# Packing w_in by chunk with mirrored blocks, and folding the row DFT twice, in a fused spectral and gated-MLP kernel

## The chip, the cores and the metric

The kernel runs on one core of one Trainium2 chip. The metric is the device time of one execution in microseconds (us), median over timed executions. TensorE is called PE in the profile, its weight loads PEld, VectorE is DVE, ScalarE is ACT, GpSimd is POOL, and SyncE, which issues most DMAs, is SP. A PSUM tile is a buffer that this kernel's matmuls write and another engine reads out before it is written again. A line number such as L477 is a line of that version's source, so the same statement has different numbers in different versions.

## The reference, cut to what matters

```python
xn = layernorm(x)                          # x is 2048 x 576, bf16
s  = irfft2(rfft2(xn) * W)                 # spectral branch, W is 2048 x 289, complex
z  = gelu(xn @ w_in)                       # w_in is 576 x 4608
z1, z2 = z[:, :2304], layernorm(z[:, 2304:])
g  = w_sp @ z2 + b_sp[:, None]             # w_sp is 2048 x 2048
out = x + s * silu((z1 * g) @ w_out)       # w_out is 2304 x 576
```

The change touches the layernorm of `x`, the first step of `rfft2` (a DFT along the 576 columns), the product with `w_in`, and one place in the last phase.

## The kernel before: the parts that matter

The 2048 rows are handled in 16 groups of 128, which this document calls rows 0 to 15. For each row DVE computes the layernorm, the normalized row is transposed (on PE for rows 0 to 6, by DMA from row 7 on) into `xnT`, DVE folds it, and PE does the DFT products, with chunks of `xn @ w_in` between them to keep PE filled. The 576 columns are two halves of H = 288; each half is cut into two blocks of 128 and a tail of 32, so `xnT` has five column blocks.

```python
# the first loads (cut)
for a, eng in enumerate((nc.sync, nc.scalar)):        # row 0, in two halves, on two queues
    eng.dma_start(out=XC[0][:, 0, a * H2:(a + 1) * H2], in_=xv[:, 0, a * H2:(a + 1) * H2])
load_win_main(*wh[0], nc.scalar, (0,))                # w_in for chunk 0: pieces, 768-byte runs
nc.scalar.dma_start(out=ident[:], in_=cd_id.ap())     # identity for the PE transposes
load_win_main(*wh[1], nc.scalar, (0,))
load_win_main(*wh[0], nc.sync, (1,))
load_row(1)
load_row(2)
...
def ln1_apply(m):                                     # DVE: one instruction of 512 columns, one of 128
    nc.vector.tensor_scalar(out=xn[:, 0:4 * P]..., in0=xr[:, :, 0:2 * P]..., scalar1=mean, scalar2=rs, ...)
    nc.vector.tensor_scalar(out=xn[:, 4 * P:KS * P]..., in0=xr[:, None, :, 2 * P:H2]..., ...)

def p0_fold(m):                                       # DVE: column j plus and minus column j + H
    xe, xo = xnT[:, m, 0:KS - 1:2, :], xnT[:, m, 1:KS - 1:2, :]
    nc.vector.tensor_tensor(out=FS[m % 4][:, 0, :, :], in0=xe, in1=xo, op=ALU.add)
    nc.vector.tensor_tensor(out=FS[m % 4][:, 1, :, :], in0=xe, in1=xo, op=ALU.subtract)

def p0(m, start):                                     # PE: four matmuls of 2 * LE = 290 columns
    for par in range(2):                              # even and odd frequencies
        for k in range(2):                            # two blocks of 128
            nc.tensor.matmul(p0_ps[m][:, par, 0:2 * LE], lhsT=FS[m % 4][:, par, k, :], rhs=CDSD[:, par, k, :], ...)
...
# the loop over rows (cut): DVE works ahead of PE
for m in range(MT):
    if m > 1: p0_fold(m)
    if m + 5 < MT: ln1(m + 5)                         # statistics
    if m + 4 < MT: ln1_apply(m + 4)
    ...                                               # PE: chunks of xn @ w_in; p0(m, ...)
...
# the gating phase, one unit (cut): `later` holds the last row's finish, g*y and then +x, on DVE
prod(b, "P6", tb[u, 0])
add(p1a, b, p1)
while later:
    later.pop()()
tsum(u + 1, 0)
...
add(p1, b, p1b)
u_sum(1, 1, c, p1)                                    # frees the PSUM tile c
```

## Time and profile before

The time before is 493.46 us (median of 3 runs, 493.25 to 493.56). The head of its profile page reads as follows. The busy line gives the busy time of each engine, its share of the span, and its number of instructions; the line with percentages alone is the chain of work that ended last, by engine; the last line is DMA traffic by packet size.

```profile
span 491.6 us, 9285 instructions
...
PE 483.9 (98%) x3407; PEld 306.1 (62%) x3407; DVE 331.7 (67%) x739; ACT 159.8 (33%) x335; POOL 206.4 (42%) x272
...
DMA packets 94605, 72.13 MB, mean 147 GB/s; under 512 B 45920, under 2 KB 86752, under 8 KB 94304
...
PE 96%; DVE 1%; ACT 1%; DMA 1%; issue 0%; SPq 0%; DVEq 0%
```

PE bounds the kernel. So a saved PE column is worth its time, unless PE then waits for something.

The start is the one stretch where PE waits. This is PE's timeline of the kernel before: start, duration, engine, line, operation, count, and in brackets the idle time in front and what ended it.

```profile
1.21 3.68 PE L756 MATMUL pw<-Z_74 128*128 128x512 bf16 x9 [1.21 <-DVE Z_74 L220]
5.98 0.44 PE L320 MATMUL pt<-ident,AR 128*128 128x128 bf16 x5 [1.09 <-DMA ident<-c_id]
6.25 0.38 PE L761 MATMUL pw<-Z_74 128*128 128x512 bf16 x1
7.25 0.82 PE L477 MATMUL ph<-AR 128*128 128x384 bf16 x4 [0.62 <-DVE AR L324]
```

Nine warm-up matmuls, row 0's transposes as soon as the identity has landed, and the first chunk of `xn @ w_in` (L477) at 7.25 us.

```profile
32.31 0.66 PE L348 MATMUL pa<-AR 128*128 128x290 bf16 x4
...
33.58 0.67 PE L348 MATMUL pa<-AR 128*128 128x290 bf16 x4
...
36.69 0.66 PE L348 MATMUL pa<-AR 128*128 128x290 bf16 x4
...
37.95 0.67 PE L348 MATMUL pa<-AR 128*128 128x290 bf16 x4
```

PE is busy without a gap, DVE for 6.56 of 10 us (4.82 of the first five, 1.74 of the last). From start to start the 290-column matmuls take 122 to 134 ns. DVE's fold of row 9 ends 2.15 us before its product starts; that distance, DVE's lead over PE, is 0.41 us at row 3, 2.98 at row 8, 2.15 at row 9, 3.37 at row 10 and 2.75 at row 11.

One more place: in the last phase, the finish (multiply and add, L695 and L696) sits on DVE in front of the add that frees a PSUM tile, and PE loses about 0.3 us between the matmuls at 417.94 and 419.08 us.

```profile
416.80 0.45 DVE L695 TENSOR_TENSOR AR<-AR 128x576 bf16<-128x576 bf16 x1
...
417.28 0.81 DVE L696 TENSOR_TENSOR AR<-AR 128x576 bf16<-128x576 bf16 x1
...
419.08 1.03 PE L636 MATMUL pm<-AR 128*128 128x256 bf16 x8
```

### The profile page before, as it was taken

The page shows a single profiled execution, that of the slowest core. Times are in us where ns is not written, and L with a number is a line of the kernel's source. Part 1 is how long each engine was busy: PE and PEld are TensorE (multiplying, and loading weights), DVE is VectorE, ACT ScalarE, POOL GpSimd, SP SyncE. Part 2 cuts the span into 40 slices and gives each one's busy share as a digit, 9 for nine tenths or more (in the row PEclk, how much of TensorE's full clock was granted, in tenths as well). Part 3 has the DMA queues.
Part 4 walks back from the last instruction along what each step waited for, and adds up shares of the span by engine and source line. Part 5 has one row for each costly group of instructions (what it writes and reads, how often), then busy time and mean ns, then how long its engine had stood idle before and what let it go on. Part 6 is the DMA issues. An engine that isn't in the chain of part 4 may idle for free.

```text
span 491.6 us, 9285 instructions
## 1 busy us (share of the span) xinstructions
PE 483.9 (98%) x3407; PEld 306.1 (62%) x3407; DVE 331.7 (67%) x739; ACT 159.8 (33%) x335; POOL 206.4 (42%) x272
## 2 busy tenths in 40 slices
PE   7999999999999999999999999999999999999996
PEld 3555454555556444566666677666666678888885
DVE  6995378798876989856656627666566426877632
ACT  4777777867767565200000111000000011000001
POOL 3681134424533794455354301553553312666600
PEclk9999999999999999999999999999999999999999
DMA  8878899978574999851111896111211872111212
GB/s 272 243 138 201 232 314 274 346 222 225 158 247 113 259 265 252 263 177 33 47 50 34 173 184 170 45 33 34 64 33 39 170 173 70 56 44 44 71 37 61
DMA packets 94605, 72.13 MB, mean 147 GB/s; under 512 B 45920, under 2 KB 86752, under 8 KB 94304
## 3 DMA queue, kind: packets, MB, share of 16 engines
q1 hardware_dynamic: 88832, 57.88, 45.6%
q0 software_dynamic: 4896, 13.17, 8.3%
q8 instruction: 26, 0.43, 0.4%
q10 hardware_dynamic: 832, 0.50, 0.3%
q14 instruction: 19, 0.16, 0.1%
HBM read 40.40 MB, written 21.26 MB: 125 GB/s over the span
## 4 chain that ended last, share of the span: by engine, by line
PE 96%; DVE 1%; ACT 1%; DMA 1%; issue 0%; SPq 0%; DVEq 0%
PE pm L636 44%; PE ph L477 15%; PE ph L573 14%; PE po L690 13%; PE pa L348 2%; PE pb L405 2%; PE pa L421 1%; PE pa L447 1%; PE pa L369 1%; PE pl L690 1%; PE pa L393 1%; DMA AR<-in_A_x_dram 1%; PE pa L440 0%; PE pa L340 0%; PE pt L320 0%; ACT AR L353 0%
## 5 line engine op out<-in xcount | busy, mean ns | idle before, releaser
L636 PE MATMUL pm<-AR,Z_74 128*128 128x384 bf16 (+1 forms) x864 | 138.8, 308 | 0.0
L640 DVE TENSOR_TENSOR AR<-pm,AR 128x384 f32<-128x384 f32 (+3 forms) x162 | 82.4, 513 | 73.4 <-PE pm L636 69.8
L636 PEld LDWEIGHTS <-Z_74 128*128 128x128 bf16 x864 | 84.5, 98 | 40.6
L636 PE MATMUL pm<-AR 128*128 128x384 bf16 (+1 forms) x648 | 107.0, 308 | 0.1
L477 PE MATMUL ph<-AR 128*128 128x384 bf16 (+1 forms) x480 | 87.2, 327 | 0.7 <-DVE AR L324 0.6
L573 PE MATMUL ph<-AR 128*128 128x512 bf16 (+1 forms) x360 | 84.7, 379 | 0.0
L636 PEld LDWEIGHTS <-AR 128*128 128x128 bf16 x648 | 63.4, 98 | 30.7 <-issue 0.3
L650 ACT ACTIVATE AR<-pm 128x384 f32<-128x384 f32 (+1 forms) x27 | 12.3, 455 | 185.3 <-PE pm L636 185.3
L690 PE MATMUL po<-AR 128*128 128x288 bf16 x540 | 66.6, 286 | 0.0
L690 PEld LDWEIGHTS <-AR 128*128 128x128 bf16 x594 | 56.9, 98 | 13.9
L477 PEld LDWEIGHTS <-AR 128*128 128x128 bf16 (+1 forms) x480 | 39.6, 97 | 38.7 <-issue 16.7
L624 POOL TENSOR_TENSOR AR<-Z_74,AR 128x1024 bf16<-128x1024 bf16 x26 | 55.3, 2126 | 12.8 <-PE pm L636 11.4
L651 POOL TENSOR_TENSOR AR<-AR 128x384 f32<-128x384 f32 (+1 forms) x27 | 22.9, 849 | 81.0 <-ACT AR L650 78.4
L593 POOL DMA_DIRECT2D Z1d<-AR x55 | 32.0, 583 | 56.8 <-ACT AR L582 54.5
L582 ACT ACTIVATE AR<-ph 128x512 bf16<-128x512 f32 x72 | 41.9, 596 | 19.8 <-PE ph L573 19.6
L573 PEld LDWEIGHTS <-AR 128*128 128x128 bf16 (+1 forms) x360 | 30.3, 97 | 27.6 <-issue 4.1
L496 ACT ACTIVATE Z_74<-ph 128x384 bf16<-128x384 f32 x72 | 33.6, 499 | 20.1 <-PE ph L477 19.7
L654 POOL TENSOR_TENSOR AR<-AR 128x384 f32<-128x384 f32 (+1 forms) x27 | 30.3, 1123 | 11.8 <-DVE AR L640 11.8
L693 ACT ACTIVATE AR<-po 128x576 bf16<-128x576 f32 x15 | 9.8, 651 | 76.7 <-PE po L690 76.7
L695 DVE TENSOR_TENSOR AR<-AR 128x576 bf16<-128x576 bf16 (+2 forms) x18 | 7.6, 424 | 39.9 <-ACT AR L693 39.9
L647 DVE TENSOR_TENSOR AR<-AR 128x384 bf16<-128x384 bf16 (+1 forms) x108 | 31.7, 334 | 0.9
L395 DVE TENSOR_TENSOR AR<-pa,AR 128x578 bf16<-128x578 f32 x32 | 22.8, 752 | 6.4 <-PE pa L393 3.9
(188 smaller groups left out, 457.6 us busy)
## 6 DMA issues: line engine op xcount, KB each, us to landing
Z1d<-AR POOLq DMA_DIRECT2D x55, 128.0 KB, 4.1
AR<-Z1d SPq DMA_DIRECT2D x36, 192.0 KB, 3.0
AR<-in_A_x_dram SPq DMA_DIRECT2D x19, 144.0 KB, 3.1
AR<-in_B_w_in_dram SPq DMA_DIRECT2D x14, 192.0 KB, 3.8
AR<-in_B_w_out_dram SPq DMA_DIRECT2D x1, 2592.0 KB, 11.5
AR<-Ad SPq DMA_DIRECT2D x4, 578.0 KB, 7.8
AR<-in_A_w_r_dram SPq DMA_DIRECT2D x16, 144.5 KB, 3.9
AR<-in_A_w_i_dram SPq DMA_DIRECT2D x16, 144.5 KB, 3.8
```

What stands on the lines that cost most here:

```text
L477: nc.tensor.matmul(self.ph[:], lhsT=xnT[rows, self.m, ks, :], rhs=WIN2[rows, ks, n * ZC:(n + 1) * ZC], start=start, stop=stop)
L496: nc.scalar.activation(out=zc, in_=ph[:], func=ACT.Gelu_apprx_tanh)
L573: nc.tensor.matmul(self.ph[:].rearrange("p (a t) -> p a t", a=4), lhsT=wb[rows, ks, (fi % WG) * P:(fi % WG + 1) * P], rhs=xnT[rows, 4 * tq ...
L582: nc.scalar.activation(out=zs, in_=ph[:], func=ACT.Gelu_apprx_tanh)
L593: (nc.sync if place[0] > len(kinds) - 16 else nc.gpsimd).dma_start(out=d, in_=s_)
L624: (nc.gpsimd if u else nc.vector).tensor_tensor(out=t, in0=zblk(p, 1, 0), in1=t2, op=ALU.subtract)
L636: nc.tensor.matmul(dst, lhsT=z[:, s, :], rhs=SLB[SA[name]][:, s, 0:nt], start=(s == 0 and not more), stop=(s == HM - 1), skip_group_check= ...
L640: nc.vector.tensor_tensor(out=out, in0=x, in1=y, op=ALU.add)
L647: nc.vector.tensor_tensor(out=o, in0=o, in1=zb[:, f, h, 0:nt], op=ALU.mult)
L651: nc.gpsimd.tensor_tensor(out=p1b, in0=p1, in1=B[1], op=ALU.add)
L654: nc.gpsimd.tensor_tensor(out=ux, in0=p1a, in1=B[0], op=ALU.add)
L690: nc.tensor.matmul(pv[:, hh, :], lhsT=U[:, fi, h, i * P:(i + 1) * P], rhs=WOUT[:, fi, c0 + hh * H2:c0 + hh * H2 + w // nh], start=(fi == 0 ...
```

## The change

The intent has three parts. First, the host lays `w_in` out by chunks of 384 columns, so that one chunk is one DMA with runs of 3840 bytes per partition, where it took up to six DMAs with runs of 768 bytes (of 1536 where two chunks came together). Second, the second block of each half is mirrored (column H-1-i in place of 128+i). A DFT along mirrored pairs splits once more: the sum of a pair needs the cosine columns alone for even frequencies, the difference the sine columns, and the other way round for odd ones. So from row 8 on DVE folds a second time, and PE multiplies by 145 columns in each of its four matmuls instead of 290. Third, some things were moved: the order of the first loads, half of row 1's statistics, the statistics of row 6, and the finish in the last phase.

```diff
+def pack_w_in(w, zc=384):
+    D, F = w.shape
+    H = D // 2
+    nt_ = H - 2 * P
+    i = np.arange(P)
+    rows = np.stack([i, H + i, H - 1 - i, 2 * H - 1 - i, i // nt_ % 2 * H + P + i % nt_], axis=1)
+    return np.ascontiguousarray(w[rows].reshape(P, rows.shape[1], F // zc, zc).transpose(2, 0, 1, 3))
 ...
-    for a, eng in enumerate((nc.sync, nc.scalar)):
-        eng.dma_start(out=XC[0][:, 0, a * H2:(a + 1) * H2], in_=xv[:, 0, a * H2:(a + 1) * H2])
-    load_win_main(*wh[0], nc.scalar, (0,))
+    load_win2(0, nc.scalar)                      # one DMA of 480 KB
     nc.scalar.dma_start(out=ident[:], in_=cd_id.ap())
-    load_win_main(*wh[1], nc.scalar, (0,))
-    load_win_main(*wh[0], nc.sync, (1,))
-    load_row(1)
-    load_row(2)
-    load_win_main(*wh[1], nc.sync, (1,))
+    nc.scalar.dma_start(out=WIN2[:, 1, 0:3, :], in_=B_w_in[NZC + 1, :, 0:3, :])
+    for m in range(3):
+        load_row(m)
+    nc.sync.dma_start(out=WIN2[:, 1, 3:KS, :], in_=B_w_in[NZC + 1, :, 3:KS, :])
 ... (the later loads likewise, one DMA per chunk)
     def ln1_apply(m):
-        nc.vector.tensor_scalar(out=xn[:, 0:4 * P]..., in0=xr[:, :, 0:2 * P]..., ...)
+        for b in range(2):
+            nc.vector.tensor_scalar(out=xn[:, 2 * b * P:2 * (b + 1) * P]...,
+                                    in0=xr[:, :, H2 - 1:H2 - 1 - P:-1] if b else xr[:, :, 0:P], ...)
 ...
     def p0_fold(m):
 ...
+        if m >= FD0:
+            for c, op in enumerate((ALU.add, ALU.subtract)):
+                nc.vector.tensor_tensor(out=FD[m % 4][:, c, :, :], in0=FS[m % 4][:, :, 0, :], in1=FS[m % 4][:, :, 1, :], op=op)
+    FD0 = 8
 ...
     def p0(m, start):
         for par in range(2):
-            for k in range(2):
+            for c in range(2 * (m >= FD0)):
+                nc.tensor.matmul(p0_ps[m][:, par, c * LE:(c + 1) * LE], lhsT=FD[m % 4][:, c ^ par, par, :],
+                                 rhs=CDSD[:, par, 0, c * LE:(c + 1) * LE], ...)
+            for k in range(2 * (m < FD0)):
                 nc.tensor.matmul(p0_ps[m][:, par, 0:2 * LE], lhsT=FS[m % 4][:, par, k, :], ...)
 ...
-        while later:
+        while later and not u:
             later.pop()()
         tsum(u + 1, 0)
 ...
         add(p1, b, p1b)
         u_sum(1, 1, c, p1)
+        while later:
+            later.pop()()
 ...
         ln1(0)
+        ln1_stats(1, (0,))
         ln1_recip(0)
         ln1_apply(0)
-        ln1(1)
+        ln1_stats(1, (1,))
+        ln1_aggr(1)
 ... (and the statistics of row 6 split around ln1_apply(5))
```

More of the change, by code (lines that the diff above doesn't have):

```diff
@@ L29, in build_consts @@
     d = np.zeros((3, P))
-    for b in range(2):
-        d[b] = b * P + np.arange(P)
+    d[0] = np.arange(P)
+    d[1] = H - 1 - np.arange(P)
     nt_ = H - 2 * P
-    d[2, 0:nt_] = 2 * P + np.arange(nt_)
+    d[2, 0:nt_] = P + np.arange(nt_)
     d[2, nt_:2 * nt_] = H + d[2, 0:nt_]
@@ L105 @@
     _, S, D = A_x.shape
-    F = B_w_in.shape[1]
-    Fh = F // 2
+    Fh = B_w_out.shape[0]
     L = D // 2 + 1
@@ L176 @@
     FS = [reg("G4", i * 4 * P, 4 * P).rearrange("p (a b t) -> p a b t", a=2, b=2) for i in range(4)]
+    FD = [reg("G4", (i + 4) * 4 * P, 4 * P).rearrange("p (a b t) -> p a b t", a=2, b=2) for i in range(4)]
     G1 = reg("A0", KS * 2 * L, N2 * P).rearrange("p (s k) -> p s k", s=N2)
@@ L191 @@
     WIN1 = [reg("WI", i * KS * WG * P, KS * WG * P).rearrange("p (k f) -> p k f", k=KS) for i in range(2)]
-    WIN2 = reg("RW", 0, KS * Fh).rearrange("p (k f) -> p k f", k=KS)
+    WIN2 = reg("RW", 0, KS * Fh).rearrange("p (n k f) -> p n k f", n=NZC, k=KS)
     xnT = reg("XT", 0, MT * KS * P).rearrange("p (m k t) -> p m k t", m=MT, k=KS)
@@ L227, with load_win2 @@
     HT = H2 - 2 * P
-    wv = B_w_in.rearrange("(a d) f -> a d f", a=2)
-    def load_win_main(t, fs, eng=nc.sync, halves=(0, 1)):
-        for a in halves:
-            eng.dma_start(out=t[:, a:KS - 1:2, :], in_=wv[a, 0:2 * P, fs].rearrange("(b p) f -> p b f", p=P))
-    def load_win_tail(t, fs, eng=nc.sync):
-        for q in range(4):
-            eng.dma_start(out=t[q * HT:(q + 1) * HT, KS - 1, :], in_=wv[q % 2, 2 * P:H2, fs])
-    def load_win(t, fs):
-        load_win_main(t, fs)
-        load_win_tail(t, fs)
-    def load_win1(g):
-        fs = slice((g % (FT // WG)) * WG * P, (g % (FT // WG) + 1) * WG * P)
-        wb = WIN1[g % 2]
-        load_win(wb, fs)
-    for a, eng in enumerate((nc.sync, nc.scalar)):
-        eng.dma_start(out=XC[0][:, 0, a * H2:(a + 1) * H2], in_=xv[:, 0, a * H2:(a + 1) * H2])
-    wh = [(WIN2[:, :, n * ZC:(n + 1) * ZC], slice(Fh + n * ZC, Fh + (n + 1) * ZC)) for n in range(2)]
+    def load_win1(g):
+        nc.sync.dma_start(out=WIN1[g % 2], in_=B_w_in[g % (FT // WG)])
+    def load_win2(n, eng=nc.sync):
+        eng.dma_start(out=WIN2[:, n, :, :], in_=B_w_in[NZC + n])
     def load_row(m):
         nc.sync.dma_start(out=XC[0][:, m, :], in_=xv[:, m, :])
-    load_win_main(*wh[0], nc.scalar, (0,))
+    load_win2(0, nc.scalar)
     nc.scalar.dma_start(out=ident[:], in_=cd_id.ap())
-    load_win_main(*wh[1], nc.scalar, (0,))
+    nc.scalar.dma_start(out=WIN2[:, 1, 0:3, :], in_=B_w_in[NZC + 1, :, 0:3, :])
     nc.scalar.activation(out=THF[:, 1:2], in_=eps[:], func=ACT.Sqrt)
-    load_win_main(*wh[0], nc.sync, (1,))
-    load_row(1)
-    load_row(2)
-    load_win_main(*wh[1], nc.sync, (1,))
-    for g in range(3):
-        third = (WIN2[:, :, 2 * g * ZC:2 * (g + 1) * ZC], slice(Fh + 2 * g * ZC, Fh + 2 * (g + 1) * ZC))
-        if g:
-            load_win(*third)
-        else:
-            load_win_tail(*third, nc.gpsimd)
-            load_row(3)
-            nc.sync.dma_start(out=CDSD, in_=cd_cdsd.ap().rearrange("p (a k l) -> p a k l", a=2, k=3))
+    for m in range(3):
+        load_row(m)
+    nc.sync.dma_start(out=WIN2[:, 1, 3:KS, :], in_=B_w_in[NZC + 1, :, 3:KS, :])
+    load_row(3)
+    nc.sync.dma_start(out=CDSD, in_=cd_cdsd.ap().rearrange("p (a k l) -> p a k l", a=2, k=3))
+    load_x(1)
+    for g in range(1, 3):
+        load_win2(2 * g)
+        load_win2(2 * g + 1)
         load_x(g + 1)
@@ L305, in ln1_apply @@
         xr = XC[m // 4][:, m % 4, :].rearrange("p (a d) -> p a d", a=2)
-        nc.vector.tensor_scalar(out=xn[:, 0:4 * P].rearrange("p (b a i) -> p a b i", b=2, a=2),
-                                in0=xr[:, :, 0:2 * P].rearrange("p a (b i) -> p a b i", b=2), scalar1=mean, scalar2=rs,
-                                op0=ALU.subtract, op1=ALU.mult)
+        for b in range(2):
+            nc.vector.tensor_scalar(out=xn[:, 2 * b * P:2 * (b + 1) * P].rearrange("p (a i) -> p a i", a=2),
+                                    in0=xr[:, :, H2 - 1:H2 - 1 - P:-1] if b else xr[:, :, 0:P], scalar1=mean, scalar2=rs,
+                                    op0=ALU.subtract, op1=ALU.mult)
         nc.vector.tensor_scalar(out=xn[:, 4 * P:KS * P].rearrange("p (r a i) -> p r a i", r=2, a=2),
-                                in0=xr[:, None, :, 2 * P:H2].to_broadcast((P, 2, 2, HT)), scalar1=mean, scalar2=rs,
+                                in0=xr[:, None, :, P:P + HT].to_broadcast((P, 2, 2, HT)), scalar1=mean, scalar2=rs,
                                 op0=ALU.subtract, op1=ALU.mult)
@@ L346, in p0 @@
         for par in range(2):
-            for k in range(2):
+            for c in range(2 * (m >= FD0)):
+                nc.tensor.matmul(p0_ps[m][:, par, c * LE:(c + 1) * LE], lhsT=FD[m % 4][:, c ^ par, par, :],
+                                 rhs=CDSD[:, par, 0, c * LE:(c + 1) * LE], start=start and c == 0, stop=not start,
+                                 skip_group_check=True)
+            for k in range(2 * (m < FD0)):
                 nc.tensor.matmul(p0_ps[m][:, par, 0:2 * LE], lhsT=FS[m % 4][:, par, k, :], rhs=CDSD[:, par, k, :],
@@ L476, in mm @@
             n = self.n
-            nc.tensor.matmul(self.ph[:], lhsT=xnT[rows, self.m, ks, :], rhs=WIN2[rows, ks, n * ZC:(n + 1) * ZC],
+            nc.tensor.matmul(self.ph[:], lhsT=xnT[rows, self.m, ks, :], rhs=WIN2[rows, n, ks, :],
                              start=start, stop=stop)
@@ L805 @@
             if m + 5 < MT:
-                ln1(m + 5)
+                ln1_stats(m + 5, (0, 1) if m != 1 else (0,))
+                if m != 1:
+                    ln1_aggr(m + 5)
             if m + 4 < MT:
                 ln1_apply(m + 4)
+                if m == 1:
+                    ln1_stats(m + 5, (1,))
+                    ln1_aggr(m + 5)
                 if m + 4 >= DT:
@@ L937 @@
             a = a.astype(_np.int64)
+        if name == "B_w_in":
+            a = pack_w_in(a)
         arrays[f"in_{name}_dram"] = a
```

## The prediction

> **What bounds it now.** The tensor engine: the page's busy table gives PE 483.9 of 491.6 us (98%), the chain of waits is 96% PE, the granted clock 1.00. Counting only time between matmul starts that exceeds their columns, after 20 us PE loses about 0.1 us per group of four chunks and 0.3 us at 418.7 us (timeline), no more. Before 20 us it loses about 5.7 us: 1.2 before the first matmul, 1.7 of slow warm-up matmuls, 2.0 waiting for row 0's layernorm, identity and transposes (4.5 to 7.25 us), the rest small waits, mostly on DVE. From 3 to 20 us the DMA engines are full (windows: about 350 GB/s), and DVE is 85 to 99% busy from 5 to 35 us.
>
> **DFT (the main term, all critical).** In rows 8 to 15 four matmuls of 290 columns become four of 145. In the timeline four of 290 take 0.49 us from start to start; the inverse transform's four of 144, with equal weight loads, 0.26. So 0.24 us per row, 8 rows: 1.9 us.
>
> **DVE (added).** Two more folds per row from row 8 on: today's take 0.205 us from start to start, so +0.41 us per row. The normalization of 512 columns (0.28 us to the next start) becomes two of 256, about 0.21 each [...]. [...] DVE spends about 1.9 us per row against PE's 2.19; then about 2.1, and in rows 8 to 10 about 2.5 against PE's 1.95. Its lead over PE (fold done to DFT start) is 0.3 us at row 3, 3 us at row 8. It may run out near rows 3 to 5 and 9 to 11. I charge 0.4 us of new PE waits.
>
> **Loads.** Same bytes, but one DMA of 3840-byte runs in place of up to six of 768. After 20 us that is worth nothing: no matmul waits for it. At the start row 1 comes right after row 0 (it landed at 5.76 us; DVE waited 0.55), and the identity, for which the first transpose waited until 5.93, stands behind 480 KB of weights. [...] With half of row 1's statistics moved into the 0.37 us wait for the square root, I expect the first z2 matmul 0.4 us sooner, near 6.9.
>
> **Output tail.** At 416 to 419 us the deferred finish (0.9 us of DVE) delays the add that frees a PSUM bank. Moving it behind that add removes 0.3 us.
>
> **Sum.** 493.5 - 1.9 - 0.4 - 0.3 + 0.4 = 491.3; I say 491.1 us, 8 in 10 between 489.6 and 492.4. Faster by over 2% (9.9 us): 0.01; within 2%: 0.98; slower: 0.01.
>
> **What would show it.** 145-column matmuls about 62 ns apart. [...] First z2 matmul near 6.9 us. No PE gap over 0.2 us near 416 us. Packets and DMA issues well down, to no effect on PE after 20 us.
>
> **What would make it wrong.** A slow mirrored read or late row 0 starving PE in the first 20 us (up to +1.5); DVE running out at rows 9 to 11 (up to +1); weight loads holding 145-column matmuls near their 98 ns (gain only 0.8). On the other side, the loads might free more of the 3 us that PE waits between 4.5 and 20 us, down to 489.

The 0.4 us of new PE waits was the author's estimate; two instructions at about 0.21 us where one took 0.28 is 0.14 us more per row, and the 0.21 is an estimate too, near the 0.205 us of the 256-column folds.

## More of the kernel before

The share of 67% for DVE is an average over the whole span, and the rows are all done in the first 50 us; from 5 to 35 us DVE is busy for 28.1 of 30 us, 94%.

DVE's first statistics had waited 1.8 us for row 0 of `x`; this line is from the view of waits in 0 to 9 us (total, times, longest):

```profile
DVE st_131 L282 <- DMA AR<-in_A_x_dram: 1.8, 1, 1.8
```

The rows are the stretch that the change aims at. Here is one window of it (length; busy time and count of PE, PEld, DVE, ACT, POOL; PE clock; DMA share; GB/s), then PE's timeline of the DFT products of rows 8 to 11:

```profile
30.00:40.00 10.00, 10.00 (x74) 5.90 (x72) 6.56 (x26) 7.22 (x15) 7.79 (x13) 1.00 0.88 163
```

## The result, and the profile after

The changed kernel took 495.99 us (median of 4 runs, 495.76 to 497.28) against 493.37 of the kernel before in the same rounds. A ratio here is the mean time of one kernel's runs over the mean of the other's of the same rounds, so it is not quite the ratio of the quoted medians. It is 1.0058 (95% interval 1.0040 to 1.0076): 2.6 us slower by the medians where 2.4 us faster was predicted, and outside the predicted range of 489.6 to 492.4.

The head of its page, whose profile fell on the slowest of its runs:

```profile
span 495.2 us, 9258 instructions
...
PE 485.0 (98%) x3407; PEld 306.2 (62%) x3407; DVE 338.6 (68%) x771; ACT 160.1 (32%) x335; POOL 203.9 (41%) x268
...
DMA packets 89228, 72.12 MB, mean 146 GB/s; under 512 B 45216, under 2 KB 79904, under 8 KB 88928
...
PE 89%; DVE 7%; DMA 2%; ACT 1%; issue 1%; POOL 0%; SPq 0%; DVEq 0%; ACTq 0%; POOLq 0%
```

The chain now runs through DVE for 7% of the span, which was 1%. The DMA packets are fewer by 5,377. The busy time of PE is no measure of its work here: it rose although columns went away, because it contains matmuls that ran at half rate, as the last of the three PE lines below shows. The timeline of PE's start, and the one wait for row 0 of `x`:

```profile
6.63 0.77 PE L311 MATMUL pt<-ident,AR 128*128 128x128 bf16 x5 [1.41 <-DVE AR L297]
7.19 0.64 PE L763 MATMUL pw<-Z_74 128*128 128x512 bf16 x1
8.08 1.46 PE L477 MATMUL ph<-AR 128*128 128x384 bf16 x4 [0.25 <-DVE AR L315]
```

```profile
DVE st_117 L272 <- DMA AR<-in_A_x_dram: 3.5, 1, 3.5
```

The four matmuls of L477 take 1.46 us where they took 0.82, and they start 0.83 us later. Row 0 is awaited 3.5 us and not 1.8. The identity no longer matters (it landed at 5.61): the transposes wait for DVE's normalization, which had waited for row 0.

The window in the rows, and the DFT products of rows 8 to 11:

```profile
30.00:40.00 10.00, 9.55 (x77) 5.48 (x75) 9.76 (x40) 6.59 (x14) 7.00 (x13) 1.00 0.61 130
```

```profile
34.34 0.42 PE L344 MATMUL pa<-AR 128*128 128x145 bf16 x4
...
35.72 0.57 PE L344 MATMUL pa<-AR 128*128 128x145 bf16 x4 [0.28 <-DVE AR L326]
...
38.73 0.42 PE L344 MATMUL pa<-AR 128*128 128x145 bf16 x4
...
40.94 0.57 PE L344 MATMUL pa<-AR 128*128 128x145 bf16 x4 [1.11 <-DVE AR L326]
```

The 145-column matmuls start 62 to 74 ns apart where they don't wait, so four of them save 0.24 us, as predicted. But DVE is busy 9.76 of 10 us, and PE waits for the second fold (L326) at rows 9 and 11. Counted as the time between matmul starts beyond what their columns take, these two waits are 0.45 and 1.28 us. DVE's lead is 1.07 us at row 8, then -0.15, 0.24 and -0.15; a lead of about -0.15 us means that PE was waiting.

The normalization of one row on DVE, first before, then after the change; the next instruction follows 0.28 us after the one of 512 columns, and 0.47 us after the first of the two of 256:

```profile
32.33 0.37 DVE L306 TENSOR_SCALAR AR<-AR,mv_562,rs 128x512 bf16<-128x512 bf16 x1
...
32.61 0.31 DVE L309 TENSOR_SCALAR AR<-AR,mv_562,rs 128x128 bf16<-128x128 bf16 x1
```

```profile
34.16 0.56 DVE L297 TENSOR_SCALAR AR<-AR,mv_529,rs 128x256 bf16<-128x256 bf16 x2
...
34.63 0.31 DVE L300 TENSOR_SCALAR AR<-AR,mv_529,rs 128x128 bf16<-128x128 bf16 x1
```

The last phase, with the finish in its new place (L697, L698):

```profile
421.58 2.12 POOL L624 TENSOR_TENSOR AR<-Z_74,AR 128x1024 bf16<-128x1024 bf16 x1 [0.17 <-PE pm L636]
...
422.39 1.63 DVE L697 TENSOR_TENSOR AR<-AR 128x576 bf16<-128x576 bf16 x1
...
424.06 0.46 DVE L698 TENSOR_TENSOR AR<-AR 128x576 bf16<-128x576 bf16 x1
...
427.45 1.03 PE L636 MATMUL pm<-AR 128*128 128x256 bf16 x8 [0.64 <-DVE AR L640]
```

The wait was not removed. It is 0.80 us where it had been 0.28, a few microseconds later. The multiply took 1.63 us, which was 0.45 us before.

Three suspects, then, all of them PE waits that the change made: the second fold, the first loads, and the finish. A fourth is the half rate of those matmuls, at a granted clock that the record gives as 1.00 from 8 to 12 us.

### The profile page after: what moved, and what is told of

Read it like the earlier page. It is cut to its first block, busy times and chain, and to the rows that moved or that the text cites. A ratio compares the mean times of both kernels' runs of the same rounds, so it can differ in the third digit from the quotient of the medians.

```text
span 495.2 us, 9258 instructions
## 1 busy us (share of the span) xinstructions
PE 485.0 (98%) x3407; PEld 306.2 (62%) x3407; DVE 338.6 (68%) x771; ACT 160.1 (32%) x335; POOL 203.9 (41%) x268
## 4 chain that ended last, share of the span: by engine, by line
PE 89%; DVE 7%; DMA 2%; ACT 1%; issue 1%; POOL 0%; SPq 0%; DVEq 0%; ACTq 0%; POOLq 0%
PE pm L636 43%; PE ph L573 14%; PE po L692 13%; PE ph L477 11%; PE pb L405 2%; DVE AR L297 1%; DMA AR<-in_B_w_in_dram 1%; PE pa L421 1%; PE pa L447 1%; PE pa L369 1%; PE pl L692 1%; PE pa L393 1%; DMA AR<-in_A_x_dram 1%; DVE AR L300 1%; DVE AR L322 0%
## 5 line engine op out<-in xcount | busy, mean ns | idle before, releaser
L477 PE MATMUL ph<-AR 128*128 128x384 bf16 (+1 forms) x480 | 89.1, 333 | 0.2 <-DVE AR L315 0.2
L477 PEld LDWEIGHTS <-AR 128*128 128x128 bf16 (+1 forms) x480 | 39.9, 98 | 38.7 <-issue 17.6
L624 POOL TENSOR_TENSOR AR<-Z_74,AR 128x1024 bf16<-128x1024 bf16 x26 | 55.3, 2127 | 13.6 <-PE pm L636 12.3
L697 DVE TENSOR_TENSOR AR<-AR 128x576 bf16<-128x576 bf16 (+2 forms) x18 | 9.7, 541 | 39.9 <-ACT AR L695 39.9
L700 POOL DMA_DIRECT2D out_dram<-AR x12 | 6.6, 548 | 49.9 <-DVE AR L698 33.8
```

Of the source, the lines that this page charges most:

```text
L477: nc.tensor.matmul(self.ph[:], lhsT=xnT[rows, self.m, ks, :], rhs=WIN2[rows, n, ks, :], start=start, stop=stop)
L624: (nc.gpsimd if u else nc.vector).tensor_tensor(out=t, in0=zblk(p, 1, 0), in1=t2, op=ALU.subtract)
```

## The experiments

In each table of this section "before" is the kernel before in the same rounds of the same chip. Times can be compared inside a batch; between batches (chips 15, 4, 15, 15 and 7) the same changed kernel gave ratios of 1.0058 and 1.0036, so differences below 1 us between batches are read from the traces alone. Where a trace is used, it is one profiled run.

### First batch: undo one part each

The theory: the second fold from row 8 on costs PE as much in waits as it saves in columns; the late row 0 and the moved finish make the rest. The rival for the first part is that the waits come from somewhere else (loads, the DMA transposes) and stay without the second fold.

No second fold at all, everything else as changed:

```diff
-    FD0 = 8
+    FD0 = 16
```

> The changed kernel with the second fold taken away from all rows (threshold 16): DFT products of 290 columns in every row, everything else kept. Theory D (VectorE runs out: the second fold costs 0.41 us of VectorE per row in rows 8 to 11 on top of 0.19 us of the split normalization, and PE waits for the fold at rows 9 and 11, 0.45 and 1.28 us; late VectorE also delays the DMA transposes and so the 1 MB constant load behind them, which delays the z1 weights, 1.07 us at 56.6 us): both row waits vanish and the wait at 56.6 us shrinks below 0.3 us; PE loses 1.9 us of DFT gain; total within 1 us of the changed kernel, 495 to 496.5. Rival S (the late start carries through: row 0 landed 1.6 us later, and the waits at rows 9 and 11 are that lateness seen later): waits at rows 9 and 11 stay in some form, and total rises by the whole 1.9 us to about 498.

The second fold from row 12 on:

```diff
-    FD0 = 8
+    FD0 = 12
```

> The changed kernel with the second fold in rows 12 to 15 only. Theory D: VectorE has nothing else in those rows, so no wait at rows 8 to 11; half of the DFT gain (0.96 us) is kept; 1.0 to 2.5 us faster than the changed kernel, 493.5 to 495. Rival S: waits at rows 9 and 11 stay, total 0.9 us slower than the changed kernel.

Row 0 of `x` in two halves at the head of both queues, as before:

```diff
+    for a, eng in enumerate((nc.sync, nc.scalar)):
+        eng.dma_start(out=XC[0][:, 0, a * H2:(a + 1) * H2], in_=xv[:, 0, a * H2:(a + 1) * H2])
     load_win2(0, nc.scalar)
 ...
-    for m in range(3):
+    for m in range(1, 3):
         load_row(m)
```

> The changed kernel with the old order of the first loads: row 0 in two halves at the head of the two queues, the weights behind it. If the 480 KB weight load at the head of the other queue is what made row 0 land at 4.58 us instead of 2.95, row 0 lands near 3 us, the first z2 matmul starts 0.8 us or more sooner (by 7.3 us), PE no longer runs its first 24 z2 matmuls at half rate, and the total falls 0.8 to 3 us (493 to 495.2). Theory D: the waits at rows 9 and 11 stay (1.5 us or more together). Rival S: they vanish and the total falls by over 3 us.

The finish back at its old place:

```diff
-        while later and not u:
+        while later:
             later.pop()()
 ...
-        while later:
-            later.pop()()
```

> The changed kernel with the deferred output finish back at its old place, before the first T sum of the next unit. The changed kernel has a PE wait of 0.80 us at 426.5 us where the old one has 0.28 at 418.7; one VectorE multiply of the finish took 1.63 us there, while GpSimd ran its 2.1 us T sum. If that overlap is the cause, the multiply is back under 0.9 us, the PE wait is back to about 0.3 us, and the total falls 0.4 to 0.6 us. If the wait was chance or of other origin, no change.

| kernel | median us (range) | ratio to before (95%) |
|---|---|---|
| before | 493.48 (492.92 to 494.89) | |
| no second fold (x1_fd16) | 494.90 (494.69 to 495.65) | 1.0032 (1.0020 to 1.0044) |
| second fold from row 12 (x2_fd12) | 494.66 (493.75 to 495.02) | 1.0020 (1.0006 to 1.0033) |
| row 0 in halves first (x3_row0) | 494.92 (494.77 to 496.26) | 1.0029 (1.0017 to 1.0041) |
| finish at its old place (x4_later) | 495.22 (494.52 to 495.45) | 1.0033 (1.0021 to 1.0045) |

The changed kernel itself did not run in this batch. Against its first ratio of 1.0058 all four gain, against the 1.0036 that it gave later only the second clearly tends to. From the start of row 8's DFT to the start of row 15's, the kernel before takes 14.39 us. Without the second fold it is 14.39 as well, with it from row 12 on 13.68, and with it from row 8 on 14.55 (the kernel with the finish moved back, 14.56). So in those rows the second fold saves 0.7 us when it starts at row 12 and nothing when it starts at row 8. The waits at rows 9 and 11 are there in every kernel with a start at row 8 (0.44 and 1.26 to 1.29 us in the two others of this batch) and in none with a later start. This is PE's timeline of the kernel with the second fold from row 12, around its rows 9 and 11; no bracket, no wait:

```profile
34.78 0.67 PE L348 MATMUL pa<-AR 128*128 128x290 bf16 x4
...
39.15 0.67 PE L348 MATMUL pa<-AR 128*128 128x290 bf16 x4
```

That settles the rival: loads and transposes were the same, and the waits went with the second fold of rows 8 to 11.

With the finish at its old place the multiply took 0.45 us again and PE's wait was 0.28 us, against 0.80 in the three others of the batch. From the start of the last third of the gating phase to PE's end it took 73.14 us, as in the kernel before, and not 73.74. In its timeline:

```profile
418.06 0.45 DVE L695 TENSOR_TENSOR AR<-AR 128x576 bf16<-128x576 bf16 x1
...
418.54 0.81 DVE L696 TENSOR_TENSOR AR<-AR 128x576 bf16<-128x576 bf16 x1
```

So the move costs 0.6 us by the traces: in all twenty, the stretch takes 73.13 or 73.14 us with the old place and 73.73 to 73.96 with the new one. The multiply takes 1.62 or 1.63 us in each of the nine with the new place. In its new place it falls into GpSimd's sum L624, which runs from 421.58 to 423.70 us: it ended at 424.02, 0.32 us after that. The profiles before and after hold 60 of the finish's multiplies and adds at 576 columns. Four of them started while a GpSimd TENSOR_TENSOR was running: they took 0.81 to 1.63 us, and each ended 0.31 or 0.32 us after it (the add L696 at 417.28 in the kernel before is one, 0.81 us). The 56 others took 0.45 or 0.46 us.

Row 0 in halves landed at 2.92 and 3.09 us, where the whole row had landed between 4.38 and 5.20. The first chunk then started at 7.44, but in this kernel the first transpose waited 1.09 us for the identity (landed 6.07). Against what was expected of this run, half rate did not go away: it came from 8.10 to 11.5 us.

### Second batch: the rest of the start, the layout alone, and another order on DVE

The identity ahead of the weights, with row 0 in halves:

```diff
+    for a, eng in enumerate((nc.sync, nc.scalar)):
+        eng.dma_start(out=XC[0][:, 0, a * H2:(a + 1) * H2], in_=xv[:, 0, a * H2:(a + 1) * H2])
-    load_win2(0, nc.scalar)
     nc.scalar.dma_start(out=ident[:], in_=cd_id.ap())
+    load_win2(0, nc.scalar)
 ...
-    for m in range(3):
+    for m in range(1, 3):
         load_row(m)
```

> The changed kernel with row 0 in two halves at the head of both queues and the identity right behind its half, before the first 480 KB of weights. In the run with row 0 alone moved forward, row 0 landed at 2.92 us but the identity at 6.07, and the first transpose stood until 6.1. Theory L (the start is lost to the order of the loads, row 0 and identity behind the weights): the identity lands before 4.5 us, the first transpose starts near 5.1, the first z2 matmul near 6.6 (7.25 in the kernel before, 8.08 in the changed one), PE loses 1 us less or more in the first 10 us, total 1 to 2 us below the changed kernel. Rival W (the first weights, one 480 KB piece, are what the first z2 matmul then waits for): they land near 5.5, so no; if they do, it shows as a PE wait for that DMA after the transposes. The waits at rows 9 and 11 stay.

Eight more warm-up matmuls in front, to separate the half-rate matmuls from the waits:

```diff
         for i in range(2):
-            for j in range(5 - i):
+            for j in range(9 - i):
                 nc.tensor.matmul(pw[:], lhsT=warm[:, 0:P], rhs=warm, start=True, stop=True)
```

> The changed kernel with eight more warm-up matmuls, so that PE is not idle from 4.8 to 6.6 us. In the changed kernel every 384-column matmul from 8.4 to 12.3 us takes 158 ns longer (half rate), in the kernel before none. If the half rate comes from that idle time: the extra 158 ns are gone, PE's excess before 20 us falls by about 1.5 us, the total by 0.5 to 1.5. If it does not: the half rate stays, and the total is unchanged or longer. The row waits at rows 9 and 11 stay.

The kernel before with the packed layout alone: the old blocks (not mirrored), the old order of loads, no second fold, the old finish:

```diff
+    rows = np.stack([i, H + i, P + i, H + P + i, i // nt_ % 2 * H + 2 * P + i % nt_], axis=1)
+    return np.ascontiguousarray(w[rows].reshape(P, rows.shape[1], F // zc, zc).transpose(2, 0, 1, 3))
 ...
-    load_win_main(*wh[0], nc.scalar, (0,))
+    load_win2(0, slice(0, 2), nc.scalar)
 ... (each other piece at the start likewise; later one DMA per chunk)
```

> The kernel before with nothing changed but the layout of the input weights: chunk by chunk, with the old block order, the same order of the first loads, one DMA for each later chunk. No fold, no mirrored blocks. My theory: the bytes are the same and no matmul after 20 us waits for weights, so 0.3 us at most either way against the kernel before (493.1 to 493.8), with thousands of packets fewer. Rival: the layout itself costs, because a 480 KB piece lands whole (the z1 weights at 55 us land later than their first halves did), 0.5 us or more slower, with a PE wait for that DMA near 55 us.

The changed kernel with DVE's statistics and normalization done one row later from row 8 on, which clears the folds of rows 8 to 11 of other work:

```diff
+            q = m - (m >= 8)
-            if m + 5 < MT:
-                ln1_stats(m + 5, (0, 1) if m != 1 else (0,))
+            if q + 5 < MT and m != 8:
+                ln1_stats(q + 5, (0, 1) if q != 1 else (0,))
 ... (and so on with q for ln1_aggr, ln1_apply, xpose_dma)
```

> The changed kernel with VectorE's work of rows 8 to 12 handed on by one row: in row 8 no statistics and no normalization, from row 9 on those of one row earlier than in the changed kernel (rows are still normalized three ahead). Same instructions, another order. Theory D (VectorE has no room for the second fold in rows 8 to 11, while it idles in rows 12 to 15): the waits of 0.45 and 1.28 us before the DFT of rows 9 and 11 vanish, total 1 to 2 us below the changed kernel. Rival: the wait is the length of the chain transpose, fold, second fold, matmul within one row, not VectorE's load; then the waits stay, as the chain is as long.

| kernel | median us (range) | ratio to before (95%) |
|---|---|---|
| before | 493.58 (493.24 to 494.02) | |
| identity first, row 0 in halves (y1_ident) | 495.91 (493.99 to 496.91) | 1.0044 (1.0028 to 1.0061) |
| more warm-up (y2_warm) | 495.21 (494.93 to 496.23) | 1.0037 (1.0025 to 1.0049) |
| packed layout alone (y3_pack) | 492.97 (492.63 to 493.46) | 0.9990 (0.9978 to 1.0002) |
| normalization one row later (y4_shift) | 495.91 (495.10 to 496.26) | 1.0042 (1.0029 to 1.0055) |

With the identity first, the first transposes ran at 5.69 us, 0.9 us before those of the changed kernel, and nothing was gained: the first weights (480 KB in one DMA) now landed at 7.99 (4.91 in the profile after), and the first chunk started at 8.13 and then waited again for the second chunk's weights. In these runs the queue heads traded row 0, the identity and the first weights against each other.

In the profile after, PE ran at half rate until 12.7 us: at half rate a chunk's matmul takes 320 ns from start to start and not 162. With more warm-up no matmul after 5.5 us ran at half rate, and the time stayed that of the changed kernel. In its trace the stretch from the first chunk to row 2's DFT takes 12.03 us; the changed kernel, run again in the fourth batch and at half rate from about 7.5 to 11 us, takes 12.02. Both have the same median, 495.2 us, though in different batches. So in that stretch the half rate is hidden under the waits for DVE. Only the first profile after had more (12.73). So the half rate is not what makes the changed kernel's median slower.

The packed layout alone is at or a little below the kernel before; its interval touches 1. Its trace spends 138.76 us from the first spectral matmul to the first gating matmul, which was 139.12 in the kernel before. Ten of the nineteen traces with the packed layout have this 138.76; the nine others have single waits of 0.3 to 1.1 us there. But there is one trace of the kernel before, and matched matmul by matmul its 0.36 us is two waits of PE, 0.23 us at 68.47 and 0.13 at 102.79. The first comes from ACT, which started late on a copy:

```profile
67.76 0.65 ACT L371 ACTIVATE AR<-pa 128x578 bf16<-128x578 f32 x1 [0.88 <-PE pa L369]
```

The profile puts its wait down to PE, but the store issued at 60.84, which had to free the buffer, landed at 67.66. In y3_pack that store took 4.97 us and not 6.82, and ACT did not wait for it. The fourth batch shows the same wait, and longer, in kernels with the packed layout. So these traces do not show that the layout saves anything.

Shifting the normalization moved the waits and did not remove them: none at row 9, 0.81 us at row 13 and 0.29 at row 15. Row 9's chain of transpose, fold, second fold and matmul is as long as before, so its length alone does not explain the wait there. DVE itself then waited for a DMA transpose. From its view of waits in 30 to 50 us:

```profile
DVE AR L321 <- DMA AR<-AR: 1.9, 1, 1.9
PEld L344 <- DVE AR L326: 1.6, 3, 0.9
```

In rows 8 to 11 of the changed kernel DVE needs about 2.6 us per row and PE 1.95. An order on DVE can only use up the lead that it has built by row 8, and that is smaller now.

### Third batch: the old start and old finish, and where the second fold may begin

All four have the packed layout and mirrored blocks, with the start loads of y3_pack, the old order of the first layernorms and the old finish. Row 6's statistics stay split, as in the changed kernel. They differ in the second fold: from row 11, none, from row 8, and from row 8 with rows 8 to 11 on GpSimd.

```diff
-    FD0 = 8
+    FD0 = 11
 ... (old start, old finish)
```

> The changed kernel (packed weights, mirrored blocks, split normalization) with three of its parts set back or cut: the first loads in small pieces over three queues in the old order and row 1's statistics behind row 0's normalization (as in the run with the layout alone), the deferred finish at its old place, and the second fold from row 11 on. In the run without second fold VectorE's lead over PE is 1.83 us at row 10 and 1.02 at row 11; the fold takes 0.54 until it is done, so no row waits. DFT gain 5 x 0.24 = 1.2 us, start as in the layout run (492.97), 0.19 us per row of normalization on VectorE costing 0.2 to 0.5 of PE early: 492.0 to 492.6, below both kernels.

```diff
-    FD0 = 11
+    FD0 = 16
```

> The same without any second fold. Against the layout run it has only the mirrored blocks, with the normalization in three VectorE instructions per row for two. Theory: that costs VectorE 0.19 us per row, which PE feels only in the first 20 us, where it waits for the normalization of rows 2 to 6: 0.2 to 0.8 us above the layout run, 493.2 to 493.8. VectorE's lead at row 8 falls from 3.0 us to about 1.6 with no wait there. Rival: the late start alone made that loss in the changed kernel; then equal to the layout run, lead 3.0.

```diff
-    FD0 = 11
+    FD0 = 8
```

> The same with the second fold from row 8 on, as in the changed kernel. Theory D: the lead at row 8 is about 1.1 us, rows 9 and 11 wait for the fold, 0.4 and 1.3 us, although the start is back to the old one; so 0.5 us or more above the run with the fold from row 11 on, about 493. Rival S: with the old start no wait at rows 9 and 11, and 0.7 us below that run, 491.5.

```diff
-                nc.vector.tensor_tensor(out=FD[m % 4][:, c, :, :], ...)
+                (nc.gpsimd if m < 12 else nc.vector).tensor_tensor(out=FD[m % 4][:, c, :, :], ...)
 ...
-    FD0 = 11
+    FD0 = 8
```

> The same with the second fold from row 8 on, but in rows 8 to 11 its two instructions on GpSimd. Theory D: VectorE has its room back; if GpSimd needs about 0.6 us for each (its 1024-element T sum takes 2.13 us), rows 9 and 11 wait less than with the fold on VectorE, total 491.5 to 492.5. If GpSimd is full there (it makes the row's inverse root and issues a store per row, 1.6 us of about 2), the normalization gets later instead and rows 10 to 13 wait: 493 or more.

| kernel | median us (range) | ratio to before (95%) |
|---|---|---|
| before | 493.25 (493.00 to 494.53) | |
| from row 11 (z1_fd11) | 493.27 (492.64 to 495.33) | 1.0001 (0.9985 to 1.0017) |
| none (z2_fd16) | 493.73 (493.31 to 494.21) | 1.0006 (0.9993 to 1.0019) |
| from row 8 (z3_fd8) | 493.72 (493.43 to 494.95) | 1.0009 (0.9996 to 1.0022) |
| rows 8 to 11 on GpSimd (z4_pool) | 495.31 (495.20 to 495.34) | 1.0037 (1.0025 to 1.0049) |

With the old start and the old finish the second fold from row 8 on costs and gains about nothing, and the two waits are still there, in a kernel whose start is as early as before. So they do not come from the late start:

```profile
34.10 0.57 PE L349 MATMUL pa<-AR 128*128 128x145 bf16 x4 [0.28 <-DVE AR L331]
...
39.34 0.57 PE L349 MATMUL pa<-AR 128*128 128x145 bf16 x4 [1.13 <-DVE AR L331]
```

From row 8's DFT to row 15's it takes 13.45 us with the second fold from row 11, 14.38 without it, and 14.59 with it from row 8. From row 11 on the fold gains 0.93 us; from row 8 on it loses 0.2. The timed differences of the first three are inside each other's intervals, and the first missed its 492.0 to 492.6.

Comparing the kernel without the second fold with y3_pack isolates the mirrored blocks, but for the split of row 6's statistics. From the first chunk to row 2's DFT it takes 12.03 us against 11.57, and from there to row 8's 13.60 against 13.41: 0.65 us in all, with DVE's lead at row 3 gone from 0.41 to -0.14 us and at row 8 from 3.01 to 1.61. The timed ratios differ by 0.0016, about 0.8 us, though they are from two batches. Two instructions of 256 columns take 0.47 us to the next start where one of 512 took 0.28: 0.19 us more per row. The mirrored read itself is not slow: in the profile after it took 0.34 us in 15 of the 16 rows, and the plain one beside it 0.30 to 0.35 in 14. What costs is the second instruction: in rows 7 to 14 the plain one alone takes 0.22 us to the next start, for half of the columns that took 0.28 together, and the mirrored one 0.26. Why half the columns take more than half the time no run here shows.

GpSimd takes 0.66 us for one of these instructions, where DVE's take 0.29. It was worse than DVE; from the view of waits in 30 to 45 us:

```profile
PEld L349 <- POOL AR L331: 4.6, 7, 1.1
```

PE waited seven times, 0.35 to 0.91 us each.

### Fourth batch: can a combination beat the kernel before, and the changed kernel again

The kernel with the second fold from row 11, with six more warm-up matmuls:

```diff
-            for j in range(5 - i):
+            for j in range(7 - i):
 ...
-        keep_warm(1)
+        keep_warm(3)
```

> The run with the second fold from row 11 on (old first loads, old finish), plus six warm-up matmuls: four before the first transpose, two between it and the first z2 matmul. In that run PE had 158 ns more per matmul from 9.2 to 12 us (half rate) in the profile, and its times spread from 492.64 to 495.33. If idle time of PE before 8 us brings the half rate on: no half rate, 492.0 to 492.7, spread under 1 us, clear of the kernel before by 0.7 us or more. If not: no change, 493.3.

The packed layout alone, with the same six:

```diff
-            for j in range(5 - i):
+            for j in range(7 - i):
 ...
-        keep_warm(1)
+        keep_warm(3)
```

> The kernel before with the layout alone, plus the same six warm-up matmuls. The layout run showed no half rate in its profile, so little is to be won: 492.6 to 493.1. Against the run with the fold from row 11 on and the same warm-up it says what mirrored blocks and fold are worth net in rows that have room: DFT gain 1.2 us less 0.8 us for the split normalization, so that run should be 0.2 to 0.6 us faster.

The changed kernel with only the first loads and row 1's statistics set back:

```diff
-    load_win2(0, nc.scalar)
+    for a, eng in enumerate((nc.sync, nc.scalar)):
+        eng.dma_start(out=XC[0][:, 0, a * H2:(a + 1) * H2], in_=xv[:, 0, a * H2:(a + 1) * H2])
+    load_win2(0, slice(0, 2), nc.scalar)
 ... (the other pieces likewise)
-        ln1_stats(1, (0,))
 ...
-        ln1_stats(1, (1,))
-        ln1_aggr(1)
+        ln1(1)
```

> The changed kernel with only the first loads and the place of row 1's statistics set back (small pieces, three queues). Theory L: the order of the first loads is worth 1.0 to 1.8 us of its loss; total 494 to 494.8; the two row waits (0.44 and 1.28 us) and the 0.80 us wait at the start of the third gating stay. Rival: the finish and the late constant load make up the difference; then 495.3 or more.

The changed kernel as it is, for comparison in this batch (no edit):

> The changed kernel itself once more, in the same rounds as the others, because its first four times had one at 497.3 and its profile is of that one. Expected 495.3 to 496; the waits at rows 9 and 11 and at the third gating within 0.05 us of the first profile; the waits for the z1 weights at 56.6 us (1.07) and at 71 us (0.88) smaller or absent, as they were 0 in one and 0.5 and 0.7 in another run with the same fold.

| kernel | median us (range) | ratio to before (95%) |
|---|---|---|
| before | 493.48 (492.73 to 494.69) | |
| from row 11, warm (w1_best) | 493.03 (492.50 to 493.64) | 0.9994 (0.9983 to 1.0006) |
| packed layout alone, warm (w2_packwarm) | 493.21 (492.75 to 493.50) | 0.9994 (0.9982 to 1.0006) |
| changed, old start (w3_start) | 495.22 (494.25 to 495.98) | 1.0035 (1.0022 to 1.0047) |
| changed, again (w4_again) | 495.20 (494.65 to 495.70) | 1.0036 (1.0024 to 1.0048) |

No version is clear of the kernel before, and the first missed the 492.0 to 492.7 expected of it. The start set back gained nothing in time, although its first chunk ran at 7.52 us in place of 8.37. Its trace has given the time back by 70 us: ACT waited 1.68 us until a store of a spectral intermediate had landed and freed its buffer, and PE lost 1.02 us there. From ACT's timeline:

```profile
69.36 0.65 ACT L376 ACTIVATE AR<-pa 128x578 bf16<-128x578 f32 x1 [1.68 <-DMA Bd<-AR]
```

That wait is intermittent. It cost PE 0.88 us in the changed kernel's first profile and nothing in this batch's, 0.68 in x3_row0, 0.63 in y1_ident, nothing in y3_pack and, as shown above, 0.23 in the kernel before. What brings it about is not settled.

### Fifth batch: start and finish apart once more

The question left was whether the start is worth anything with the finish out of the way. Both kernels have the second fold from row 8 and the old finish. The first has the old start (it is z3_fd8 again), the second the new one (x4_later again).

```diff
 ... (z3_fd8, no edit)
```

> The changed kernel with old first loads, old place of row 1's statistics and old place of the finish (the second fold from row 8 on stays), once more, beside the next run, which differs in the first loads alone. The traces so far put the first z2 matmul 0.85 us sooner with the old first loads, and the lead is still 0.8 us at the DFT of row 15; the timed pair of the last rounds showed nothing (495.22 and 495.20), with a wait of 1.0 us near 69 us in the one profile. Theory L: 0.5 to 1.2 us below the next run, 493.5 to 494.3. Rival: the later waits for DMA give the sooner start back every time; equal within 0.3 us.

```diff
 ... (x4_later, no edit)
```

> The changed kernel with the finish alone at its old place, once more: 494.5 to 495.2, that is 0.5 to 0.6 us less than the changed kernel's 1.0036 to 1.0058 of the kernel before, as the traces have it (from the start of the third gating to PE's end 73.14 us against 73.74).

| kernel | median us (range) | ratio to before (95%) |
|---|---|---|
| before | 493.62 (493.06 to 494.35) | |
| old start, old finish (v1_start_later) | 494.07 (493.48 to 495.39) | 1.0010 (0.9995 to 1.0024) |
| new start, old finish (v2_later) | 494.81 (494.39 to 495.64) | 1.0024 (1.0011 to 1.0038) |

The medians differ by 0.7 us in favour of the old start, with intervals that overlap; in the pair of the fourth batch they differed by nothing. In the traces the first chunk started at 7.20 and 8.12 us. So the new start costs 0.85 and 0.92 us up to the first chunk in the two pairs, and between nothing and 0.7 us of the time; the traces show one way in which the rest is lost, the wait near 69 us, which v1_start_later had as well (0.81 us) and v2_later had not; v2_later's trace has 0.55 us of waits at 200 to 206 us instead. Whether it always goes with an early start these runs can't tell: z3_fd8, of the same source as v1_start_later, did not have it. Over all traces the first chunk started at 7.00 to 8.08 us with the old order of loads (ten traces, mean 7.35) and at 7.88 to 8.70 with the new one (eight, mean 8.21).

The four combinations of start and finish with the second fold from row 8, put side by side across batches: both old 1.0009 and 1.0010, new start alone 1.0033 and 1.0024, new finish alone 1.0035, both new 1.0036 (1.0058 in the first measurement). So against both old, either one costs 0.7 to 1.3 us, and the second costs little on top in time. Why they do not add is not shown, and comparisons across batches are the weaker ones.

## Why the prediction was wrong

Three of the prediction's terms failed: the waits for DVE (by 2.0 us), the start (by 1.5) and the finish (by 0.9). It had named the first two under what would make it wrong, and counted too little for them.

To set the terms against each other I take the trace of the changed kernel of the fourth batch and that of the kernel before, and the time between the starts of named matmuls in the two. The last matmul ends 1.86 us later. The medians of that batch differ by 1.7 us.

| stretch | before us | changed us | difference |
|---|---|---|---|
| start to first chunk | 7.25 | 8.37 | +1.12 |
| to row 2's DFT | 11.66 | 12.02 | +0.36 |
| to row 8's DFT | 13.40 | 13.61 | +0.21 |
| to row 15's DFT | 14.39 | 14.55 | +0.16 |
| to first spectral matmul after the rows | 11.90 | 11.67 | -0.23 |
| to first gating matmul | 139.12 | 138.76 | -0.36 |
| to the last third of the gating phase | 216.72 | 216.72 | 0.00 |
| to PE's end | 73.14 | 73.74 | +0.60 |

- **DFT, predicted -1.9 us: right.** Four matmuls take 0.24 us less from start to start, in 8 rows 1.9 us. Seven rows' share (-1.7) lies in the stretch to row 15's DFT and the last one's in the stretch after it.
- **DVE, predicted 0.4 us of new waits: the mechanism was right and the size was off.** The prediction named rows 3 to 5 and 9 to 11, and its figures for the split normalization come to 0.14 us more per row; the runs showed 0.19. But "I charge 0.4 us of new PE waits" measured about 2.4: 0.36 before row 2's DFT and 0.21 around row 3, both also in the kernel with mirrored blocks and no second fold, and 1.8 in rows 8 to 15, of which 0.44 and 1.29 at rows 9 and 11. The cost per row was nearly right: DVE was put at about 2.5 us per row in rows 8 to 10 against PE's 1.95, and it took about 2.6. What was wrong is the lead with which DVE entered those rows. The prediction took the 3 us of the kernel before; it is 1.61 with the mirrored blocks alone, because the split normalization had cost 0.19 us in each row until then, and 1.07 with row 8's own second fold. I had counted the cost per row and not its sum over the rows: by an estimate from these numbers, with 3 us of lead a deficit of 0.6 us per row lasts five rows, with 1 us less than two. No run has the second fold with the old lead, since it needs the mirrored blocks.
- **Start, predicted -0.4 us: wrong in sign.** The step that failed is "I expect the first z2 matmul 0.4 us sooner, near 6.9". The trace has it at 8.08 and 8.37. The prediction named a late row 0 under what would make it wrong, and expected a gain all the same. Row 0 landed at 4.38 to 5.20 in place of 2.95 and 3.11, so 1.3 to 2.1 us after the later half. Why one row on one queue, beside a 480 KB transfer on the other, lands so late was not shown. That moving row 0 back into halves at the heads of both queues brings it to 2.92 and 3.09 was shown. How much of the 1.1 us of this trace reaches the time is open, between nothing and 0.7 us by two timed pairs.
- **Finish, predicted -0.3 us: wrong in sign.** The step that failed is "Moving it behind that add removes 0.3 us". The move did take the finish out of the way of that add, and put it beside GpSimd's sum, where its multiply took 1.63 us in place of 0.45; the next PSUM tile waited for DVE in its turn. PE's wait grew from 0.28 to 0.80 us, and setting the finish back gave 0.28 again.
- **Loads after 20 us, "worth nothing": not shown wrong.** The 0.36 us between the rows and the gating phase is two waits in the one trace of the kernel before, and the larger one, for a store, comes and goes in packed kernels too. The timed ratios of the packed layout alone, 0.9990 and with more warm-up 0.9994, are not clear of 1.

With the measured terms the sum becomes 493.5 - 1.9 + 2.4 + 1.1 + 0.6 - 0.4 = 495.3 us, against 495.20 measured in that batch; the -0.4 stands for the two waits of the kernel before. This is an account of two traces, so it says what each stretch lost in them and not that each loss reaches the median. The first measurement's median, 495.99, was 0.8 us higher. Its profile, of its slowest run, has 0.7 us more before row 2's DFT, where PE stayed at half rate until 12.7 us, and waits near 56 us (1.07) and 69 us (0.88); the trace of the fourth batch has none of the three.

Three things stay open. The intermittent waits near 56 us (for weights that landed after they were needed: landed at 57.81, needed at 56.96) and near 69 us came in some runs and not in others; so did smaller ones, as of 0.54 us near 64 us in z1_fd11, z4_pool and w1_best. Half-rate matmuls between 7 and 14 us came in 11 of the 20 profiles and not in the others, and not in the same ones for the same source. In the trace of x3_row0 PE did 2,688 columns after its first nine warm-up matmuls, until 8.10 us, and then ran at half rate until 11.5 us; in that of the kernel before it did the same 2,688 columns up to 7.92 us and stayed at full rate. What decides between the two is not shown. The granted clock in the record showed the half rate in x3_row0 (0.57 between 8 and 12 us) and not in the profile after (1.00 there), although matmuls ran at half rate in both. And the same kernel moved by 0.002 in its ratio between batches, which is more than most single parts of this change are worth.

The change as a whole gained nothing because each of its gains was bought with work on DVE or a place in a queue that was closer to the limit than its average showed (DVE busy for 9.76 of 10 us in the rows of the profile after, against 68% over its span; 335 to 340 GB/s moved from 5 to 20 us in the kernel before, against a mean of 147). If a part is worth keeping by these runs, it is the packed layout with the old blocks and the old order of loads (0.9990, not clear of 1). With mirrored blocks the second fold pays from row 11 or 12 on (0.7 to 0.9 us in those rows), and this about repays what the mirrored blocks cost (0.65 us).

## What to carry to other kernels

When work is moved from a bounding engine to another, add up the second engine's lead row by row through the stretch, from the first row on; a cost that is small per row takes away the lead that a later, costlier stretch was to live on. Before moving an instruction out of one engine's way, look at what other engines run at the new place: here the multiply took 1.63 us beside GpSimd's sum and 0.45 us away from it. And at the head of the DMA queues ask of every transfer what it delays: here row 0 in halves landed at 2.92 and 3.09 us with the identity at 6.07 (5.61 in the profile after), and with the identity ahead of the weights the first of these landed at 7.99 us (4.91 in the profile after).
